# Centring the first 128 features inside the PSUM bank: a reordered opening of a fused state-space and feed-forward kernel

## The chip, the cores and the metric

The kernel runs on one core of a Trainium2 chip. TensorE (PE in the profile) multiplies matrices and writes its results to PSUM, a memory of eight banks; VectorE (DVE), ScalarE (ACT) and GpSimd (POOL) do the rest, and DMA queues, most of them issued from SyncE (SP), move data. The metric is the device time of one execution in microseconds (us).

## What is computed

The input x holds 2048 tokens of 512 features in bf16. Each token is layer-normalised; the result goes through a state-space layer (a projection, a linear recurrence over the tokens, a projection back) and through a gated feed-forward block of width 1376, and both are added to x:

```
xn = (x - mean(x)) / sqrt(var(x) + 1e-5)
ffn = (silu(xn @ w_gate) * (xn @ w_up)) @ w_down
ssm = 2 * real(h @ C^T) + xn * Dskip,  h_t = Lambda_bar * h_{t-1} + B_bar @ xn_t
out = x + ssm + ffn
```

The matmuls of the feed-forward block take the tokens transposed (features on the partitions, tokens along the free axis).

## The kernel before, in words

The work goes in four chunks of 512 tokens, each of four tiles of 128. What concerns us is the opening, lines 723 to 767, where the first three tiles (0, 1, 2) are brought into TensorE's form as fast as they arrive. The order on each engine is the order in which the code issues the instructions; semaphores are put in where one engine needs another's result.

For a tile `i` the opening does this. `sum_dve` (line 225) has VectorE add the two halves of the features with an accumulator, so that `sums[:, i]` holds each token's sum. `raw_mm` (line 237) multiplies each of the four blocks of 128 features by the identity, so that the bank `raw[i]` holds the tile transposed, not yet centred; the four blocks are called k = 0 to 3. `mean_mm` (line 242) multiplies the sums, broadcast, by `minus_mean` (the identity times -1/512), which gives minus the mean of every token on every partition, in 128 columns of another bank (`upb[1][0]` for tile 0, `upb[1][1]` for tile 1, `low` for tile 2); ScalarE copies these to `means[:, i]` in SBUF. `centered` (line 247) has VectorE add `means[:, i]` to blocks k0 to k1 of the raw bank and write them as bf16 to `xcT`, which shares its memory with the tile that the profile calls CF. The division by the standard deviation comes later, as a scale in ScalarE's reads of the products.

`up_mm(k, tiles)` (line 727) multiplies block k of the named tiles by row k of the up weights (`sw_mm`, line 500): two matmuls of 512 columns for each tile, one for each of the two groups of output features (`upb[i][0]` and `upb[i][1]`). Four rows k = 0 to 3 add up in a bank. Banks are shared: the two banks of tile 2's projections are `raw0` (the raw bank of tile 0) and `low`, and `upb[0][0]` is also `warm`, the target of `dummy` (line 698), which multiplies constants to keep TensorE busy.

The order before is: nine dummies (four of 512 columns, five of 128); sum, raw transposes and mean of tile 0, then of tile 1; five dummies of 128 columns; the centring of block 0 of tiles 0 and 1 and of blocks 1 to 3 of tile 0; row 0 of the up weights for tiles 0 and 1; sum, raw transposes and mean of tile 2; the centring of the rest of tile 1; row 1 for tiles 0 and 1; the centring of tile 2 (block 0, then blocks 1 to 3); rows 0 and 1 for tile 2; rows 2 and 3 for all three. Then follow the statistics of the layer norm on VectorE (`ln_stats`, `ln_rstd`, with the power on GpSimd), the gate projections, and ScalarE's scaled reads (`sw_up`, line 519).

The tokens of tile 0 and the up weights come on SP's queue (lines 128 and 134), one transfer for each row k; tiles 1 and 2 come on ScalarE's queue (line 131).

Of the kernel before, what the change touches and what calls it, by code (L numbers as in the profile page):

```python
# [12 lines left out]
ALU = mybir.AluOpType  # L13
# [10 lines left out]
def kernel(  # L24
# [17 lines left out]
    nc = tc.nc  # L42
    _, L, D = A_x.shape
# [8 lines left out]
    KD = D // 128  # L52
# [25 lines left out]
    def bank(shape=(128, CW), dtype=F32):  # L78
        return psum.tile(list(shape), dtype, name="ps")
# [47 lines left out]
    minus_mean = const.tile([128, 128], BF16, name="minus_mean")  # L127
# [57 lines left out]
    def by_k(ap):  # L185
        return ap.rearrange("p (k d) -> p k d", d=128)
# [30 lines left out]
    xcT, xc = CF[:, 0], CF[:, 1]  # L217
# [5 lines left out]
    sums = const.tile([128, SW], BF16, name="sums")  # L223

    def sum_dve(i, dst):
        nc.vector.scalar_tensor_tensor(out=xnT[:, NCH - 1, i, 0:HW], in0=xall[:, i, 0:HW], scalar=1.0,
                                       in1=xall[:, i, HW:D], op0=ALU.mult, op1=ALU.add, accum_out=dst)

    raw12 = [bank() for _ in range(2)]
    low, raw0 = bank(), bank()  # L230
    upb = [[bank() for _ in range(2)] for _ in range(2)] + [[raw0, low]]
    raw = [raw0, *raw12]
    gateb = [raw12, upb[0], upb[1]]
    warm = upb[0][0]
    means = ssm.tile([128, 2, CW], F32, name="pm", bufs=3)[:, 0, 0:SW * 128].rearrange("p (i t) -> p i t", t=128)

    def raw_mm(i):
        for k in range(KD):
            nc.tensor.matmul(raw[i][:, k * 128:(k + 1) * 128], lhsT=xall[:, i, k * 128:(k + 1) * 128], rhs=ident[:],  # L239
                             start=(k == 0), stop=(k == KD - 1))  # L240

    def mean_mm(i):
        lo = (*upb[1], low)[i][:, 0:128]
        nc.tensor.matmul(lo, lhsT=sums[:, i:i + 1].to_broadcast([128, 128]), rhs=minus_mean[:], start=True, stop=True)  # L244
        nc.scalar.copy(out=means[:, i, :], in_=lo)

    def centered(i, k0, k1):
        V.tensor_tensor(out=xcT[:, k0:k1, i * 128:(i + 1) * 128], in0=by_k(raw[i][:, k0 * 128:k1 * 128]),
                        in1=means[:, i, None, :].to_broadcast([128, k1 - k0, 128]), op=ALU.add)

    def runs(ap):
        return ap.rearrange("p k (i t) -> p (k i) t", t=128)
# [18 lines left out]
    V = nc.vector  # L271
# [228 lines left out]
    def sw_mm(ps, groups, gi, i, k0=0, k1=KD):  # L500
        a, b = fgroups[gi]
        for k in range(k0, k1):
            nc.tensor.matmul(ps[:, 0:(b - a) * 128], lhsT=tokens(i, k), rhs=groups[gi][:, k, 0:(b - a) * 128],  # L503
                             start=(k == 0), stop=(k == KD - 1))
# [193 lines left out]
    def dummy(ps, n, cols):  # L698
        for _ in range(n):
            nc.tensor.matmul(ps[:, 0:cols], lhsT=one.to_broadcast([128, 128]), rhs=one.to_broadcast([128, cols]),  # L700
                             start=True, stop=True)
# [22 lines left out]
    dummy(warm, 4, CW)  # L724
    dummy(warm, 5, 128)
    nc.vector.tensor_scalar(out=minus_mean[:], in0=ident[:], scalar1=-1.0 / D, scalar2=None, op0=ALU.mult)
    def up_mm(k, *tiles):
        for i in tiles:
            for gi in ((0, 1) if i < 2 else (1, 0)):
                sw_mm(upb[i][gi], U, gi, i, k, k + 1)  # L730

    def sum_mm(i):
        sum_dve(i, sums[:, i:i + 1])
        raw_mm(i)
        mean_mm(i)

    for i in range(2):
        sum_mm(i)
    dummy(warm, 5, 128)
    for i in range(2):  # L740
        centered(i, 0, 1)
    centered(0, 1, KD)
    up_mm(0, 0, 1)
    sum_mm(2)
    centered(1, 1, KD)
    up_mm(1, 0, 1)
    for k0, k1 in ((0, 1), (1, KD)):
        centered(2, k0, k1)
    for k in range(2):
        up_mm(k, 2)  # L750
    for k in range(HK, KD):
# [194 lines left out]
```

## Time and profile before

| what | value |
|---|---|
| median of three runs | 177.8 us (177.53 to 178.41) |
| the profiled execution, its own time | 178.26 us |
| span of its instructions | 176.3 us |
| TensorE busy | 172.8 us, 98% of the span |
| VectorE busy | 158.9 us, 90% |
| ScalarE busy | 102.7 us, 58% |

The profile is of one execution. Its span goes from the first to the last instruction; the rest of that execution's own time lies around it. Matmuls are pipelined: a matmul's length in the profile is the time from its start to its modelled end, and the distance from one start to the next, its pitch, is shorter. A line such as "4.83 1.91 PE L503 MATMUL ... x4" of a listing in order of time says that four matmuls issued by line 503 began at 4.83 us and ended 1.91 us later; brackets behind a row give the idle time of that engine before it and what ended it. PEld is TensorE's loading of its stationary operand. The chain of work is followed back from the last instruction, at each step to what released it.

### The profile page before, as it was taken

How to read it: one execution, taken by the hardware profiler on the slowest of the kernel's cores; microseconds unless marked ns; L12 is line 12 of the kernel's file. 1: busy time of each engine (PE TensorE's matmuls, PEld its weight loads, DVE VectorE, ACT ScalarE, POOL GpSimd, SP SyncE). 2: the span in 40 equal slices, each digit the busy share in tenths (PEclk: the TensorE clock that was granted, in tenths of full speed). 3: DMA queues.
4: the chain of work that ended last, by engine and by line, in shares of the span. 5: the costliest groups of instructions: out<-in, count | busy, mean ns of one | idle time of the engine just before them, and what ended most of it. 6: DMA issues, size and time to landing. Idle time of an engine off the chain costs nothing.

```text
span 176.3 us, 2456 instructions
## 1 busy us (share of the span) xinstructions
PE 172.8 (98%) x896; PEld 82.3 (47%) x896; DVE 158.9 (90%) x263; ACT 102.7 (58%) x186; POOL 27.1 (15%) x36
## 2 busy tenths in 40 slices
PE   8999999999999999999999999999999999999993
PEld 4444464454444464444444444445444444444542
DVE  2699999999999999899999999999999999689642
ACT  3159879895996689976044462014766662983100
POOL 5073210032000000000302500014100000530800
PEclk9999999999999999999999999999999999999999
DMA  5994979999999600220005830006410000597741
GB/s 169 366 343 63 168 148 209 283 185 307 110 203 264 170 4 0 55 57 0 2 0 109 91 42 0 0 4 67 52 22 0 2 4 0 70 174 113 81 102 60
DMA packets 34027, 18.05 MB, mean 102 GB/s; under 512 B 24512, under 2 KB 32832, under 8 KB 33888
## 3 DMA queue, kind: packets, MB, share of 16 engines
q1 hardware_dynamic: 30128, 14.26, 35.0%
q0 software_dynamic: 3456, 3.28, 14.9%
q10 hardware_dynamic: 432, 0.36, 0.6%
q8 instruction: 7, 0.11, 0.3%
q14 instruction: 4, 0.03, 0.1%
HBM read 8.33 MB, written 5.24 MB: 77 GB/s over the span
## 4 chain that ended last, share of the span: by engine, by line
PE 98%; DVE 0%; issue 0%
PE ps L459 29%; PE ps L627 20%; PE ps L640 16%; PE ps L384 16%; PE ps L503 8%; PE ps L552 3%; PE ps L801 2%; PE ps L700 2%; PE ps L617 2%; PE ps L239 1%; PE ps L244 0%; DVE xall L643 0%; PE ps L275 0%
## 5 line engine op out<-in xcount | busy, mean ns | idle before, releaser
L426 DVE TENSOR_TENSOR_SCAN g<-r_t,car,u 128x512 bf16<-128x512 f32 x24 | 28.8, 1262 | 0.0
L640 PE MATMUL ps<-CF,wt 128*128 128x512 bf16 (+2 forms) x136 | 28.5, 367 | 0.0
L384 PE MATMUL ps<-xnT,BT 128*128 128x512 bf16 x128 | 28.1, 379 | 0.0
L627 PE MATMUL ps<-wd_sb,guT 128*128 128x512 bf16 (+2 forms) x130 | 26.6, 363 | 0.0
L459 PE MATMUL ps<-xnT,wg 128*128 128x512 bf16 x96 | 24.6, 379 | 0.0
L459 PE MATMUL ps<-xnT,wu 128*128 128x512 bf16 x96 | 24.6, 379 | 0.0
L386 ACT CAST u<-ps 128x512 bf16<-128x512 f32 x32 | 18.0, 590 | 5.7 <-PE ps L384 5.2
L486 ACT CAST u<-ps 128x512 bf16<-128x512 f32 x30 | 18.0, 599 | 5.1 <-PE ps L459 5.1
L640 PEld LDWEIGHTS <-wt 128*128 128x128 bf16 x136 | 12.8, 98 | 15.1 <-DVE xall L597 0.4
L384 PEld LDWEIGHTS <-BT 128*128 128x128 bf16 x128 | 12.5, 98 | 14.9
L627 PEld LDWEIGHTS <-guT 128*128 128x128 bf16 x130 | 12.4, 98 | 13.9
L199 POOL TENSOR_TENSOR rstd<-ve,neg_half 128x1 f32<-128x1 f32 (+1 forms) x7 | 7.0, 1003 | 73.0 <-DVE ve L198 73.0
L649 ACT CAST res<-ps 128x512 bf16<-128x512 f32 x12 | 6.9, 583 | 18.6 <-PE ps L640 18.6
L589 ACT ACTIVATE xr<-xall,nb,rstd 128x512 bf16<-128x512 bf16 x16 | 11.8, 804 | 8.6 <-DVE xall L597 5.0
L650 POOL DMA_DIRECT2D out_dram<-res x12 | 10.5, 1042 | 36.0 <-ACT res L649 30.0
L459 PEld LDWEIGHTS <-wu 128*128 128x128 bf16 x96 | 9.4, 98 | 11.3
L485 ACT ACTIVATE guT<-ps 128x512 bf16<-128x512 f32 x20 | 12.0, 600 | 4.0 <-PE ps L459 3.6
L459 PEld LDWEIGHTS <-wg 128*128 128x128 bf16 x96 | 9.4, 98 | 10.6
L212 ACT ACTIVATE xn<-xall,nb,rstd 128x512 bf16<-128x512 bf16 x8 | 6.2, 816 | 8.2 <-DVE nb L202 8.2
L459 PE MATMUL ps<-xnT,w_end 128*128 128x512 bf16 x48 | 10.8, 379 | 0.0
L189 DVE BATCH_NORM_STATS2 stats<-xall 128x6 f32<-128x512 bf16 x16 | 10.8, 676 | 0.0
L394 DVE TENSOR_TENSOR pm<-g,c 128x2048 bf16<-128x2048 bf16 x8 | 9.8, 1221 | 0.1
(129 smaller groups left out, 237.8 us busy)
## 6 DMA issues: line engine op xcount, KB each, us to landing
out_dram<-in_A_x_dram SPq DMA_DIRECT2D x8, 192.0 KB, 3.2
out_dram<-res POOLq DMA_DIRECT2D x12, 128.0 KB, 3.1
out_dram<-xall POOLq DMA_DIRECT2D x3, 512.0 KB, 6.1
wd_sb<-in_B_w_down_dram SPq DMA_DIRECT2D x1, 1280.0 KB, 8.0
wu<-in_B_w_up_dram SPq DMA_DIRECT2D x4, 256.0 KB, 4.4
wg<-in_B_w_gate_dram SPq DMA_DIRECT2D x4, 256.0 KB, 5.1
xall<-in_A_x_dram SPq DMA_DIRECT2D x1, 1024.0 KB, 7.0
xall<-in_A_x_dram SPq DMA_DIRECT2D x1, 512.0 KB, 6.5
```

The costliest lines, as they stand in the source:

```text
L189: nc.vector.bn_stats(out=stats[:, n, 0, :], in_=xall[:, n, :])
L384: nc.tensor.matmul(ps[:] if c else by_k(ps[:]), lhsT=BT[:, part, k, q * 128:(q + 1) * 128], rhs=xnT[:, c, k, :] if c else xnT0[:, k], star ...
L386: nc.scalar.copy(out=u_tiles[c][:, part, q, :], in_=ps[:])
L426: V.tensor_tensor_scan(out=g()[:, part, q, :], data0=r_t[:, q:q + 1].to_broadcast([128, CW]), data1=u_tiles[c][:, part, q, :], initial=ini ...
L459: nc.tensor.matmul(ps[:fs, lo:hi], lhsT=wslice(groups, fi, k), rhs=xnT[:, c, k, lo:hi], start=(k == 0), stop=(k == KD - 1))
L485: nc.scalar.activation(out=gu(c, fi, fi + 1)[:fs, 0, :], in_=psg[:fs], func=ACT.Silu)
L486: nc.scalar.copy(out=u_pair[c][:fs, fi % 2, :], in_=psu[:fs])
L503: nc.tensor.matmul(ps[:, 0:(b - a) * 128], lhsT=tokens(i, k), rhs=groups[gi][:, k, 0:(b - a) * 128], start=(k == 0), stop=(k == KD - 1))
L589: nc.scalar.activation(out=box["xr"][:], in_=xall[:, n, :], func=ACT.Identity, scale=rstd[:, n:n + 1], bias=nb[:, n:n + 1])
L627: nc.tensor.matmul(o_tiles[n, b][:, 0:hi - lo], lhsT=gu(c, fi, fi + 1)[:, 0, i * 128:(i + 1) * 128], rhs=wd_sb[:, fi, lo:hi], start=(fi == ...
L640: nc.tensor.matmul(o[:, 0:hi - lo], lhsT=w_tiles[c][:, part, q, i * 128:(i + 1) * 128], rhs=CF[:, part, q, lo:hi], start=False, stop=(part ...
L650: nc.gpsimd.dma_start(out=out_v[:, n, lo:hi], in_=res[:, lo:hi], accum_op=ALU.add)
```

## The change

The mean of a tile is now multiplied twice: once into the first 128 columns of its raw bank, where it adds to the raw transpose of block 0 (the transposes leave the accumulation open), and once into the other bank as before. Block 0 is thereby centred in PSUM and is only copied to `xcT`: by VectorE for tile 0 (`tensor_copy`), by ScalarE for tiles 1 and 2 (`first_copy`, ahead of `mean_copy`). `centered` handles blocks 1 to 3 alone. The order is changed: the raw transposes of tile 1 stand between the two halves of tile 0's row 0, its mean behind them, then the raw transposes of tile 2, tile 1's row 0, tile 0's row 1, the mean of tile 2, tile 1's row 1, and tile 2's rows 0 and 1. The five dummies behind the means become four behind tile 0's mean. The two halves of tile 2's rows come in the order 0, 1 instead of 1, 0.

```diff
     def raw_mm(i):
         for k in range(KD):
             nc.tensor.matmul(raw[i][:, k * 128:(k + 1) * 128], lhsT=xall[:, i, k * 128:(k + 1) * 128], rhs=ident[:],
-                             start=(k == 0), stop=(k == KD - 1))
+                             start=(k == 0), stop=False)
 
     def mean_mm(i):
         lo = (*upb[1], low)[i][:, 0:128]
-        nc.tensor.matmul(lo, lhsT=sums[:, i:i + 1].to_broadcast([128, 128]), rhs=minus_mean[:], start=True, stop=True)
-        nc.scalar.copy(out=means[:, i, :], in_=lo)
-
-    def centered(i, k0, k1):
-        V.tensor_tensor(out=xcT[:, k0:k1, i * 128:(i + 1) * 128], in0=by_k(raw[i][:, k0 * 128:k1 * 128]),
-                        in1=means[:, i, None, :].to_broadcast([128, k1 - k0, 128]), op=ALU.add)
+        for to, alone in ((raw[i][:, 0:128], False), (lo, True)):
+            nc.tensor.matmul(to, lhsT=sums[:, i:i + 1].to_broadcast([128, 128]), rhs=minus_mean[:], start=alone, stop=True)
+
+    def first_copy(i):
+        nc.scalar.copy(out=xcT[:, 0, i * 128:(i + 1) * 128], in_=raw[i][:, 0:128])
+
+    def mean_copy(i):
+        nc.scalar.copy(out=means[:, i, :], in_=(*upb[1], low)[i][:, 0:128])
+
+    def centered(i):
+        V.tensor_tensor(out=xcT[:, 1:KD, i * 128:(i + 1) * 128], in0=by_k(raw[i][:, 128:D]),
+                        in1=means[:, i, None, :].to_broadcast([128, KD - 1, 128]), op=ALU.add)
...
-    def up_mm(k, *tiles):
+    def up_mm(k, *tiles, groups=range(2)):
         for i in tiles:
-            for gi in ((0, 1) if i < 2 else (1, 0)):
+            for gi in groups:
                 sw_mm(upb[i][gi], U, gi, i, k, k + 1)
 
-    def sum_mm(i):
+    def sum_to(i):
         sum_dve(i, sums[:, i:i + 1])
-        raw_mm(i)
-        mean_mm(i)
-
-    for i in range(2):
-        sum_mm(i)
-    dummy(warm, 5, 128)
-    for i in range(2):
-        centered(i, 0, 1)
-    centered(0, 1, KD)
-    up_mm(0, 0, 1)
-    sum_mm(2)
-    centered(1, 1, KD)
-    up_mm(1, 0, 1)
-    for k0, k1 in ((0, 1), (1, KD)):
-        centered(2, k0, k1)
+
+    sum_to(0)
+    raw_mm(0)
+    mean_mm(0)
+    V.tensor_copy(out=xcT[:, 0, 0:128], in_=raw[0][:, 0:128])
+    mean_copy(0)
+    dummy(warm, 4, 128)
+    sum_to(1)
+    centered(0)
+    up_mm(0, 0, groups=[0])
+    raw_mm(1)
+    up_mm(0, 0, groups=[1])
+    mean_mm(1)
+    first_copy(1)
+    mean_copy(1)
+    sum_to(2)
+    raw_mm(2)
+    up_mm(0, 1)
+    centered(1)
+    up_mm(1, 0)
+    mean_mm(2)
+    first_copy(2)
+    mean_copy(2)
+    up_mm(1, 1)
+    centered(2)
     for k in range(2):
         up_mm(k, 2)
```

## The prediction

> **What bounds the kernel now.** I read the page's first two parts and the head of its fourth, which say who is busy and which engine ends last.
>
> ```profile
> PE 172.8 (98%) x896; PEld 82.3 (47%) x896; DVE 158.9 (90%) x263; ACT 102.7 (58%) x186; POOL 27.1 (15%) x36
> PE   8999999999999999999999999999999999999993
> PEclk9999999999999999999999999999999999999999
> PE 98%; DVE 0%; issue 0%
> ```
>
> TensorE is never idle to speak of, and the chain that ended last lies on it from end to end. So a pause that an edit opens in the matmul stream, or a matmul that it adds, comes out at the end in full, and work taken from VectorE or ScalarE pays only if a matmul was waiting for it. The edit lies in the first 9 us, so I read next the chain of work in order of time (start, length, piece). A piece's length divided by its count is the pitch of its matmuls; its start is set by ends and lies some 0.2 us behind the instruction's own.
>
> ```profile
> 0.78 2.40 PE ps L700 x9
> 3.18 0.03 issue
> 3.21 0.61 PE ps L239 x4
> 3.82 0.15 PE ps L244
> 3.98 0.43 PE ps L239 x4
> 4.40 0.11 PE ps L244
> 4.51 0.53 PE ps L700 x5
> 5.04 1.71 PE ps L503 x4
> 6.75 0.40 PE ps L239 x4
> 7.15 0.06 PE ps L244
> 7.21 3.05 PE ps L503 x14
> 25.01 13.81 PE ps L384 x64
> ```
>
> A 512-column matmul has a pitch of 1.71/4 = 0.43 us in the first group of up projections (L503), and of 13.81/64 = 0.216 us later; a 128-column one 0.53/5 = 0.107 at first and 0.06 in the mean of tile 2 (L244). So TensorE runs at half its rate until some 6.9 us and doubles there, although the page's clock row shows the full clock throughout. In the slow stretch a lost microsecond costs only half of one later, as long as the doubling stays where it is.
>
> Third, the same stretch in the order of instructions, engine by engine (start, length of the merged group, in brackets the idle time before it and its releaser).
>
> ```profile
> 3.69 0.29 PE L244 MATMUL ps<-minus_mean,sums 128*128 128x128 bf16 x1
> 4.20 0.31 PE L244 MATMUL ps<-minus_mean,sums 128*128 128x128 bf16 x1
> 4.30 0.74 PE L700 MATMUL ps<-const-bfloat16-1.0 128*128 128x128 bf16 x5
> 4.83 1.91 PE L503 MATMUL ps<-wu,CF 128*128 128x512 bf16 x4
> 6.54 0.61 PE L239 MATMUL ps<-ident,xall 128*128 128x128 bf16 x4
> 6.97 0.24 PE L244 MATMUL ps<-minus_mean,sums 128*128 128x128 bf16 x1
> 3.19 0.42 DVE L226 SCALAR_TENSOR_TENSOR xnT<-xall 128x256 bf16<-128x256 bf16 x1 [1.65 <-DMA xall<-in_A_x_dram]
> 4.31 0.29 DVE L248 TENSOR_TENSOR CF<-ps,pm 128x128 bf16<-128x128 f32 x1 [0.32 <-ACT pm L245]
> 5.52 0.41 DVE L226 SCALAR_TENSOR_TENSOR xnT<-xall 128x256 bf16<-128x256 bf16 x1
> 7.54 0.76 DVE L248 TENSOR_TENSOR CF<-ps,pm 128x128 bf16<-128x128 f32 x2 [1.13 <-ACT pm L245]
> 7.75 0.55 DVE L248 TENSOR_TENSOR CF<-ps,pm 128x384 bf16<-128x384 f32 x1
> 4.01 0.27 ACT L245 COPY pm<-ps 128x128 f32<-128x128 f32 x1 [0.94 <-PE ps L244]
> 7.24 0.27 ACT L245 COPY pm<-ps 128x128 f32<-128x128 f32 x1 [2.43 <-PE ps L244]
> 8.35 0.55 PEld L503 LDWEIGHTS <-CF 128*128 128x128 bf16 x4 [0.34 <-DVE CF L248]
> ```
>
> These give the hand-overs: mean matmul to ScalarE 0.03 us (3.69 + 0.29 to 4.01), ScalarE to VectorE 0.03 (4.01 + 0.27 to 4.31), VectorE to weight load 0.05 (7.75 + 0.55 to 8.35). The five dummies cover the wait for tile 0's first features: those are ready at 4.31 + 0.29 + 0.05 = 4.65, the dummies end at 4.83. **The mark for the sum** is 8.35: there row 1 of tile 2 starts, the last matmul that waits for a centring. Behind it the stream is gap-free.
>
> **The change, part by part.** Removed: one 128-column dummy, and three VectorE additions of 128 columns. Added: three 128-column mean matmuls into the raw banks, one VectorE copy, two ScalarE copies. Nothing is issued to a DMA queue, so SP's and POOL's queues are not touched. Net on TensorE: two matmuls of 128 columns, 2 x 0.06 = +0.12 us at the full rate, since what is added ahead of the doubling pushes other matmuls behind it. The rest is waits, so I lay the new order out, with the doubling held at 6.9.
>
> *Tile 0.* The mean into the raw bank starts at 3.69 and ends at 3.98; the second one follows at 3.80, the four dummies from 3.90 to 4.33. The copy starts on VectorE at 4.01. The trace has no copy of this shape; its bounds are
>
> ```profile
> 10.35 0.17 DVE L279 COPY prm<-ps 128x12 f32<-128x12 f32 x1
> L122 SPq DMA_DIRECT2D wu<-in_B_w_up_dram x2: 412/422/432, 1.2 to 1.7; - x2
> DMA to landing us min/median/max: 3.1/3.7/4.3
> ```
>
> 0.17 us (12 columns) below and 0.55 (the 384-column addition) above; I take 0.29, the addition of the same shape. Then the weight load can go at 4.01 + 0.29 + 0.05 = 4.35. Row 0 of the up weights (the first of these two transfers) lands at 1.2 + 3.1 = 4.3, and its hand-over lets it go at about 4.38 anyway, so a copy quicker than 0.29 gains nothing. TensorE pauses 0.05 us and starts the first up projection at 4.38 rather than 4.83. The copy stands in VectorE's queue ahead of tile 1's sum: that starts about 0.21 later (as 7.75 stands to 7.54), at 4.22 instead of 3.56, and releases its mean 0.5 later (as 3.69 to 3.19), near 4.7; tile 1's mean now waits behind two halves and four transposes, so it costs nothing.
>
> *Tile 1.* 4.38 + 0.43 + 4 x 0.107 + 0.43 = 5.66: its mean pair starts, then the raw transposes of tile 2, until 6.30. ScalarE's first copy ends at 5.66 + 0.31 + 0.03 + 0.27 = 6.28 (0.31 is what the mean at 4.20 took in a running stream at the slow rate), so tile 1's row 0 starts at 6.33, pause 0.03. Its second half straddles the doubling and ends at 7.03; row 1 of tile 0 (landed at 1.7 + 4.3 = 6.0, centred near 5.1) ends at 7.46.
>
> *Tile 2.* Its mean pair starts only now, at 7.46, where before it started at 6.97. Row 1 of tile 1 runs to 8.00. ScalarE's first copy of tile 2 starts at 7.46 + 0.24 + 0.03 = 7.73 and ends at 8.00, so row 0 goes at 8.05 (pause 0.05) and ends at 8.48. Its halves are turned round, raw bank first; the low bank is free of the mean copy when its turn comes at 8.27, or within 0.05 of that. The mean copy queues behind the first copy on ScalarE and ends at 8.27, or at 8.17 if the two overlap by 0.1, about as VectorE's do (7.54 + 0.29 against 7.75); VectorE's centring takes 0.55, and row 1 of tile 2 can go at 8.80 to 8.90. TensorE has been idle since 8.48. **This pause of about 0.37 us is the largest term**: before, six matmuls of 512 columns lay between tile 2's mean and this row, now four, and one more ScalarE copy lies in the way.
>
> Sum: 8.85 - 8.35 = **+0.50 us**, of which +0.12 is matmuls, 0.37 + 0.05 pauses at the full rate, and the rest is small pauses at the slow rate against rounding. Nothing behind takes it back:
>
> ```profile
> 8.21 0.69 DVE L189 BATCH_NORM_STATS2 stats<-xall 128x6 f32<-128x512 bf16 x1
> 9.39 0.58 POOL L199 TENSOR_TENSOR rstd<-ve,neg_half 128x1 f32<-128x1 f32 x1 [5.84 <-DVE ve L198]
> 10.63 2.42 ACT L523 ACTIVATE u<-ps,rstd 128x512 bf16<-128x512 f32 x4 [3.12 <-PE ps L503]
> ```
>
> VectorE's statistics start when the centring lets them, 0.5 later; POOL's first rstd ends near 10.5 instead of 9.97, still ahead of ScalarE's read, which moves to 11.1 with the matmuls.
>
> The profiled execution (176.3 us span, 178.26 in all, so 2.0 around it) becomes 176.8 and 178.76. It lies 0.46 over the median of 177.8 of the three runs, and I have one trace: the doubling may lie elsewhere in the others. With the doubling at 5.4 the same working gives: changed kernel, tile 1's mean at 5.53, its row 0 at 6.12 (pause 0.26), tile 2's mean at 6.98, the mark 1.39 later (as 8.85 - 7.46) at 8.37; before, tile 2's mean at 6.20 and the mark 1.38 later at 7.58; so +0.79. Between +0.50 and +0.79 I take +0.6, nearer to the trace at hand: **178.4 us**.
>
> **Rivals.**
>
> *The pauses put the doubling off (slower).* Before, the matmuls run from 3.21 with no pause over 0.05 until the rate doubles 3.7 us later. If a pause starts that count anew, the one that ends at 4.38 puts the doubling at 8.07: tile 2's mean starts at 8.04, the mark is at 8.04 + 1.39 = 9.43, +1.08, 178.9. The one at 6.33 would put it at 10.0: the mark is reached at half rate at 9.96, +1.6, 179.4. It decides from a doubling after some 7.7 on. For it: the doubling came only after the gap at 3.2. Against: transposes and mean had a pause of 0.05 at 3.64 (3.21 + 4 x 0.107 to 3.69), no shorter than the new ones, and it did not start anything anew. [...]
>
> *The up weights land later.* Before, row 0 could land 0.45 later unnoticed; now every 0.1 us shows, at half price ahead of the doubling. Landing at 4.7 gives +0.7 to +1.0, 178.5 to 178.8. For it: the cover is gone. Against: the queue ahead of it is unchanged.
>
> *Tile 2's centring is hidden after all.* If ScalarE's two copies overlap well or the banks come free earlier, only the matmuls are left, +0.12: 177.9. Against: the chain from mean to row is 1.38 us in the trace as it stands, and 4 x 0.216 cover 0.86.
>
> *The doubling comes earlier, as useful matmuls start at 4.38 (faster).* With the full rate from 4.4 on, tile 1's mean starts at 5.04, row 0 of tile 1 at 5.63, tile 2's mean at 6.51, the mark is 7.90: -0.45, 177.35. Against: the stream up to 4.3 is the same in both.
>
> **How the numbers follow.** Forecast 0.62 (178.0 to 178.8), late doubling 0.14, late weights 0.08, hidden centring 0.10, early doubling 0.06. The range goes from 177.5 (hidden centring, less the 0.4 that single runs scatter: 177.53 to 178.41) to 179.3 (late doubling at 178.9 and the same 0.4). Within 0.5% is 0.89 us, about what a measurement of this kernel can tell from no change. Slower by more: the late doubling 0.14, half the late weights 0.04, the upper end of the forecast 0.08, so 0.26. Faster by more: part of the early doubling, 0.04. Same: 0.70.
>
> **What would show it.** In the changed trace: the first up projection at about 4.4 with a pause under 0.1; tile 1's sum near 4.2; tile 2's first half of row 0 with hardly a wait; a weight load that waits 0.3 to 0.4 us for VectorE's 384-column addition of tile 2; the last row 0.5 us later than before, and from there on equal distances. A pitch of 0.43 beyond 7.7 would be the late doubling. If there is no wait ahead of row 1 of tile 2, the largest term was wrong.

## The result and the profile after

The changed kernel took 178.53 us (median of 13 runs, 178.27 to 179.07), the kernel before 177.55 in the same sessions (13 runs, 177.28 to 178.44). The ratio is 1.0044, with a 95% interval of 1.0029 to 1.0059: slower by 0.78 us (0.51 to 1.05). That is clear of scatter; the estimate lies below 0.5%, the upper end of its interval a little above. (The medians lie 0.98 apart, the means of the same runs 0.80.) The profiled execution of the changed kernel took 178.55, with a span of 176.5 us.

The chain of work of the changed kernel, in order of time (start, length, piece; pieces named after TensorE's lines 509 and 245 are the up projections and the means):

```profile
1.20 3.84 DMA wu<-in_B_w_up_dram
5.04 0.04 issue
5.08 0.38 PE ps L509
...
5.99 0.28 ACT CF L248
6.27 0.05 issue
6.31 1.04 PE ps L509 x4
7.35 0.07 PE ps L245
7.42 0.02 issue
7.44 0.27 ACT CF L248
7.71 0.18 ACT pm L251
7.88 0.02 issue
7.91 0.57 DVE CF L254
8.48 0.05 issue
8.53 1.90 PE ps L509 x8
```

Before, this stretch was TensorE alone. Now the chain leaves TensorE three times: for the transfer of the first up weights, for ScalarE's first copy of tile 1, and from tile 2's mean by way of both ScalarE copies and VectorE's centring to the mark of the prediction, row 1 of tile 2, at 8.52. TensorE's own rows say how long it stood:

```profile
3.88 0.63 PE L706 MATMUL ps<-const-bfloat16-1.0 128*128 128x128 bf16 x4
5.08 0.38 PE L509 MATMUL ps<-wu,CF 128*128 128x512 bf16 x1 [0.57 <-DMA wu<-in_B_w_up_dram]
5.30 0.38 PE L239 MATMUL ps<-ident,xall 128*128 128x128 bf16 x4
...
7.19 0.28 PE L245 MATMUL ps<-minus_mean,sums 128*128 128x128 bf16 x2
7.30 1.07 PE L509 MATMUL ps<-wu,CF 128*128 128x512 bf16 x4
8.53 1.25 PE L509 MATMUL ps<-wu,CF 128*128 128x512 bf16 x5 [0.16 <-DVE CF L254]
```

The bracket counts from the modelled end of the matmul before; by the pitch the wait is longer. The last of the four matmuls ends at 7.30 + 1.07 = 8.37 and, with a length of 0.38 and a pitch of 0.22, would have let the next start at 8.21: TensorE waited 0.32 us for tile 2's centring. And the first up projection started at 5.08, although the dummies let go at 4.30.

Two things differ between this execution and that of before which the edit does not touch, and which the runs below show to vary between executions of one kernel. The four raw transposes at 5.30 take 0.38 us together, where a slow stretch shows 0.61 to 0.63: the rate had doubled by then, not at 6.9. And row 0 of the up weights, issued at 1.20 as before, landed 3.8 us later, not 3.1.

Where the time went is settled by one subtraction. The first gate projection and the last instruction on VectorE, in the trace of before:

```profile
11.44 1.89 PE L503 MATMUL ps<-wg,CF 128*128 128x512 bf16 x8
...
173.67 0.29 DVE L643 TENSOR_TENSOR xall<-ps,jidx 128x128 bf16<-128x128 f32 x1 [0.25 <-PE ps L640]
```

and in the changed kernel:

```profile
11.61 1.67 PE L509 MATMUL ps<-wg,CF 128*128 128x512 bf16 x7
...
173.84 0.29 DVE L649 TENSOR_TENSOR xall<-ps,jidx 128x128 bf16<-128x128 f32 x1 [0.25 <-PE ps L646]
```

The distance is 162.23 in both, and between 162.22 and 162.23 in all thirteen traces of this document. So what the opening does to the time can be read from the start of the gate projections alone, and nothing later gives any of it back. These two traces differ by only 0.17, because the one of before had its doubling at 6.9, later than any other with the same transfers; the second traces below are the better pair.

### The profile page after: what moved, and what is told of

The parts are those of the page before. It is cut to its first block, busy times and chain, and to the rows that moved or that the text cites. A ratio compares the mean times of both kernels' runs of the same rounds, so it can differ in the third digit from the quotient of the medians.

```text
span 176.5 us, 2460 instructions
## 1 busy us (share of the span) xinstructions
PE 172.2 (98%) x898; PEld 81.8 (46%) x898; DVE 158.5 (90%) x261; ACT 103.0 (58%) x188; POOL 27.1 (15%) x36
## 4 chain that ended last, share of the span: by engine, by line
PE 95%; DMA 2%; DVE 0%; ACT 0%; SPq 0%; issue 0%
PE ps L465 29%; PE ps L633 20%; PE ps L646 16%; PE ps L390 16%; PE ps L509 8%; PE ps L558 3%; DMA wu<-in_B_w_up_dram 2%; PE ps L817 2%; PE ps L623 2%; DVE CF L254 0%; ACT CF L248 0%; SPq L128 0%; DVE xall L649 0%; PE ps L239 0%; ACT pm L251 0%
```

## The experiments

**The theory** ("order"): the loss is in the order of the work. Tile 2's mean is issued too late for its centring, and the first up weights have lost their cover. **Rivals**: the centring itself costs the time (three mean matmuls, ScalarE copies), or the pauses put off the doubling of TensorE's rate ("late clock"). Times below are medians beside runs of the kernel before on the same chip; a ratio of 1.001 is 0.18 us.

**The changed kernel again.** No edit.

> The changed kernel once more, for a second trace of it and its time beside the three variants on the same chip. All theories: 0.5 to 1.0 over the kernel before. Theory 'order': wherever the doubling and the first up weights lie this time, TensorE waits 0.3 to 0.6 us ahead of row 1 of tile 2 and, if row 0 of the up weights lands after 4.35, from the dummies' end until then. Rival 'late clock': a pitch of 0.43 us beyond 7.7 in this or the other trace.

178.45 us, ratio 1.0046 (1.0022 to 1.0070): +0.82. In this execution the rate doubled near 6.1 and the weights came in time:

```profile
3.84 0.63 PE L706 MATMUL ps<-const-bfloat16-1.0 128*128 128x128 bf16 x4
4.32 0.61 PE L509 MATMUL ps<-wu,CF 128*128 128x512 bf16 x1
...
7.12 0.28 PE L245 MATMUL ps<-minus_mean,sums 128*128 128x128 bf16 x2
7.24 1.07 PE L509 MATMUL ps<-wu,CF 128*128 128x512 bf16 x4
8.46 1.90 PE L509 MATMUL ps<-wu,CF 128*128 128x512 bf16 x8 [0.15 <-DVE CF L254]
```

The first up projection starts at 4.32, 0.06 after the dummies let go (3.84 + 4 x 0.107 = 4.27); from tile 2's mean to the mark it takes 8.46 - 7.12 = 1.34 us, as in the first trace (8.53 - 7.19). No pitch of 0.43 is left beyond 6.1 in either trace. That speaks against "late clock".

**The kernel before again.** No edit.

> The kernel before, unchanged, against itself: a ratio of 1.000 within 0.0015, and a second trace of it, for where the doubling of TensorE's rate and the landing of row 0 lie this time. Theory 'order': with the doubling earlier than 6.9 the mark (row 1 of tile 2) lies earlier than 8.35, by half of the difference as long as no wait comes between.

177.60 us, ratio 0.9992 (0.9974 to 1.0010). The trace shows what one execution of before had hidden:

```profile
4.81 1.43 PE L503 MATMUL ps<-wu,CF 128*128 128x512 bf16 x4
6.07 0.39 PE L239 MATMUL ps<-ident,xall 128*128 128x128 bf16 x4
6.29 0.22 PE L244 MATMUL ps<-minus_mean,sums 128*128 128x128 bf16 x1
6.35 3.21 PE L503 MATMUL ps<-wu,CF 128*128 128x512 bf16 x14
...
10.75 2.54 PE L503 MATMUL ps<-wg,CF 128*128 128x512 bf16 x11
```

The transposes of tile 2 take 0.39, so the rate had doubled by 6.07 (near 5.6 by the pitches), and the gate projections start at 10.75 instead of 11.44. The same kernel gains 0.69 us by a doubling 1.3 us earlier: half of it, as expected.

In the second trace of the changed kernel the gate projections start at 11.55, 0.80 later than here. Some 0.25 of that is chance: its rate doubled 0.5 us later, and that counts half. The estimate of 0.55 that is left agrees with the terms of the prediction: 0.32 for the wait at the mark, 0.11 for the two added matmuls of 128 columns at 0.056, and small pauses.

**Tile 2's mean earlier.** The changed kernel with one line moved:

```diff
     raw_mm(2)
+    mean_mm(2)
     up_mm(0, 1)
     centered(1)
     up_mm(1, 0)
-    mean_mm(2)
     first_copy(2)
```

> The changed kernel with one edit: tile 2's mean pair is issued straight behind tile 2's raw transposes instead of behind tile 0's row 1. Theory 'order' (the loss is the wait ahead of row 1 of tile 2, because tile 2's mean comes too late, plus the wait for the first up weights, whose cover is gone): the wait of some 0.4 to 0.5 us ahead of row 1 of tile 2 goes, the time falls by 0.4 to 0.5 from the changed kernel's and stays 0.1 to 0.5 over the kernel before. Rival 'centring itself' (the loss is the added matmuls and ScalarE copies): the time stays within 0.15 of the changed kernel's, some 0.8 over before. Rival 'late clock' (pauses put off the doubling of TensorE's rate): also as the changed kernel, and a pitch of 0.43 us still beyond 7.7 us.

177.78 us, ratio 0.9999 (0.9985 to 1.0014): 0.67 under the changed kernel's 178.45 of the same session, and level with before. The direction is as expected, the gain larger than the 0.4 to 0.5 that was expected, and nothing is left of the 0.1 to 0.5 over before. By chance this trace has the conditions of the first one of the changed kernel, an early doubling and late weights, so the two can be laid side by side:

```profile
3.68 0.52 PE L706 MATMUL ps<-const-bfloat16-1.0 128*128 128x128 bf16 x4
5.05 0.38 PE L509 MATMUL ps<-wu,CF 128*128 128x512 bf16 x1 [0.85 <-DMA wu<-in_B_w_up_dram]
...
6.28 3.63 PE L509 MATMUL ps<-wu,CF 128*128 128x512 bf16 x16
...
11.10 2.11 PE L509 MATMUL ps<-wg,CF 128*128 128x512 bf16 x9
```

Sixteen up projections follow one another from 6.28 with 3.63 us for all: (3.63 - 0.38)/15 = 0.217 each, no wait ahead of row 1 of tile 2. The first up projection starts 0.03 earlier than in the changed kernel, the gate projections 0.51 earlier (11.10 against 11.61). So the moved line is worth 0.48 us here: 0.32 is the wait at the mark, and most of the rest is the mean pair itself (0.11), which now falls into the time that TensorE waits for ScalarE's first copy of tile 1 anyway (0.24 in the first trace of the changed kernel). What makes the medians differ by 0.67 instead of 0.48 is not shown by one trace of each. The centring itself is no cause: all its instructions are still there.

**The centring alone, in the order of before.** From the first sum to tile 2's centring this kernel reads:

```python
    for i in range(2):
        sum_to(i)
        raw_mm(i)
        mean_mm(i)
    V.tensor_copy(out=xcT[:, 0, 0:128], in_=raw[0][:, 0:128])
    mean_copy(0)
    first_copy(1)
    mean_copy(1)
    dummy(warm, 4, 128)
    centered(0)
    up_mm(0, 0, 1)
    sum_to(2)
    raw_mm(2)
    mean_mm(2)
    first_copy(2)
    mean_copy(2)
    centered(1)
    up_mm(1, 0, 1)
    centered(2)
```

> Only the centring in PSUM, in the order of the kernel before: means into the raw banks, first copies by VectorE (tile 0) and ScalarE, four dummies behind both means; row 0 for tiles 0 and 1, then tile 2's transposes and means, and so on. Theory 'order': within 0.1 of the kernel before (-0.05 to +0.1), since 0.12 of added matmuls stands against the shorter way to the first row. Rival 'centring itself': about +0.8 over before, as the changed kernel. Rival 'late clock': within 0.1 of before as well, since the stream has no pause.

177.68 us, ratio 0.9987 (0.9968 to 1.0007). As the theory had it; the rival "centring itself" falls with this too. This kernel also has the changed kernel's four dummies and its turned halves of tile 2's rows, so these are not the loss either.

**The order alone, with the centring of before.** The new order of the calls; `mean_mm` and `centered` as before.

> Only the new order, with the centring of before (one mean matmul for each tile, ScalarE copies the mean, VectorE adds it to block 0 and then to blocks 1 to 3). Theory 'order': the wait for a centring is longer than in the changed kernel, since block 0 needs two hand-overs again: 0.9 to 1.3 over the kernel before, 0.2 to 0.5 over the changed one. Rival 'centring itself': within 0.15 of before. Rival 'late clock': over before by 1 us or more, with a pitch of 0.43 us beyond 7.7.

178.51 us, ratio 1.0054 (1.0029 to 1.0078): +0.96 over before, as expected, but only 0.06 over the changed kernel where 0.2 to 0.5 was expected; the intervals do not tell these apart. The trace shows the longer waits:

```profile
4.63 0.58 PE L503 MATMUL ps<-wu,CF 128*128 128x512 bf16 x1 [0.25 <-DVE CF L248]
...
6.39 1.04 PE L503 MATMUL ps<-wu,CF 128*128 128x512 bf16 x4 [0.46 <-DVE CF L248]
...
8.16 2.15 PE L503 MATMUL ps<-wu,CF 128*128 128x512 bf16 x9 [0.25 <-DVE CF L248]
```

Three waits for VectorE, of 0.25 to 0.46 by the brackets, where the changed kernel has one of 0.16. So the centring in PSUM shortens the waits that the order makes, but does not remove the last one.

**The changed kernel without the four dummies** (`dummy(warm, 4, 128)` taken out).

> The changed kernel without the four dummies behind tile 0's mean. Theory 'order': TensorE waits there for the copy and for the weights with or without them, so the time is within 0.15 of the changed kernel's (0.5 to 1.0 over before). Rival 'late clock' (a pause puts off the doubling of the rate): the pause of 0.4 us and more at 3.9 moves the doubling to 7.7 or later, and the time rises by 0.5 to 1.1 over the changed kernel's.

178.29 us, ratio 1.0023 (0.9996 to 1.0049): +0.41, a little under the 0.5 to 1.0 that was expected, in an interval that holds both the changed kernel's +0.78 and no loss at all. The rise that "late clock" asked for did not come.

```profile
3.49 0.40 PE L245 MATMUL ps<-minus_mean,sums 128*128 128x128 bf16 x2
4.17 0.61 PE L509 MATMUL ps<-wu,CF 128*128 128x512 bf16 x1 [0.28 <-DMA wu<-in_B_w_up_dram]
...
5.63 0.59 PE L239 MATMUL ps<-ident,xall 128*128 128x128 bf16 x4
6.09 1.04 PE L509 MATMUL ps<-wu,CF 128*128 128x512 bf16 x4
```

TensorE stood for 0.5 us behind tile 0's means (from 3.49 + 2 x 0.107 to 4.17), and the rate doubled near 6.05 all the same. In this trace a pause of this size did not put the doubling off to 7.7 or later.

**Centring alone, order of before, no dummies behind the means.**

> Centring in PSUM in the order of before, and none of the four dummies behind the two means. Theory 'order': the first up projection starts when row 0 of the weights and the copy are there, 0 to 0.4 earlier than with dummies; waits behind it take most of that back, so 0 to 0.2 under the kernel before. Rival 'late clock': the pause puts off the doubling, 0.3 to 1.0 over before.

177.52 us, ratio 0.9990 (0.9973 to 1.0007). The next wait took the gain back:

```profile
4.31 1.04 PE L509 MATMUL ps<-wu,CF 128*128 128x512 bf16 x4
...
6.32 3.18 PE L509 MATMUL ps<-wu,CF 128*128 128x512 bf16 x14 [0.64 <-DMA wu<-in_B_w_up_dram]
```

Row 0 starts at 4.31, 0.5 earlier than in before, and then row 1 of the weights is not there yet.

**Three attempts at an earlier row 0.** First in the changed kernel, row 0 as SP's first transfer:

```diff
-    nc.sync.dma_start(out=xall[:, 0, :], in_=x_v[:, 0, :])
+    load_row(nc.sync, wu01, wu_v, 0)
+    nc.scalar.dma_start(out=xall[:, 0, :], in_=x_v[:, 0, :])
...
-    for k in range(KD):
+    for k in range(1, KD):
         load_row(nc.sync, wu01, wu_v, k)
```

> The changed kernel with row 0 of the up weights as the first transfer on SP's queue, and tile 0's tokens moved to ScalarE's queue ahead of tiles 1 and 2. In the traces so far row 0 landed at 4.34 (before), 5.04 and 4.19 (changed, twice), 5.03 (early mean), 4.25 and 4.24. Theory 'order': the share of the loss that is the uncovered weights goes, the wait for tile 2's centring stays: row 0 lands some 0.4 us earlier, TensorE starts the first up projection within 0.1 of the dummies' end, and the time is 0 to 0.3 below the changed kernel's, 0.4 to 0.7 over before. If the weights' share is nothing: as the changed kernel, about 0.8 over before, though row 0 lands early.

179.97 us, ratio 1.0111 (1.0063 to 1.0160): a miss by 1.3 us and more. The tokens of tile 0 became the late ones:

```profile
4.14 0.61 PE L240 MATMUL ps<-ident,xall 128*128 128x128 bf16 x4 [0.96 <-DMA xall<-in_A_x_dram]
...
7.48 1.91 PE L510 MATMUL ps<-wu,CF 128*128 128x512 bf16 x4
9.19 0.42 PE L246 MATMUL ps<-minus_mean,sums 128*128 128x128 bf16 x2
```

Tile 0's transposes start at 4.14, where those of the kernels with the unedited transfers start between 3.02 and 3.23, and the up projections still run at a pitch of 0.43 at 7.48 (four in 1.91). This says nothing on the weights' share. The same in the kernel without dummies:

> The same, and row 0 of the up weights first on SP's queue, tile 0's tokens on ScalarE's. Theory 'order': 0.05 to 0.25 under the kernel before, less scatter, as the late landings of row 0 no longer count. If tile 0's tokens come later through that, the time rises by what they are late, at half price.

180.24 us, ratio 1.0120 (1.0072 to 1.0168), in the same way: tile 0's transposes start at 4.24. The half price that was expected for late tokens, some 0.5 us, is missed by far (+2.1): the rate doubled only near 9.5. Then, in the changed kernel, row 0 in two transfers:

```diff
+    for f0 in (0, FE // 2):
+        nc.sync.dma_start(out=wu01[:, 0, f0:f0 + FE // 2], in_=wu_v[:, 0, f0:f0 + FE // 2])
-    for k in range(KD):
+    for k in range(1, KD):
         load_row(nc.sync, wu01, wu_v, k)
```

> The changed kernel with row 0 of the up weights fetched in two transfers of half the features, the first half alone being what the first up projection needs; the other transfers follow 0.4 us later than they did. Theory 'order' with an uncovered first row: in traces of the same opening row 0 was issued at 1.20 and landed 2.9 to 3.1 us later in most, but 3.8 later in two (the changed kernel, early mean); the first half should land by 4.2 in all, the wait behind the dummies be under 0.15, and the time be 0 to 0.3 under the changed kernel's, that is 0.4 to 0.7 over before. If the first half lands as late as the whole row, or row 1 is late instead, as the changed kernel or over it.

179.20 us, ratio 1.0072 (1.0048 to 1.0096): +1.28 instead of 0.4 to 0.7. The first half came in time, and TensorE waited for row 1 instead:

```profile
4.10 0.61 PE L511 MATMUL ps<-wu,CF 128*128 128x512 bf16 x1
...
6.89 0.59 PE L511 MATMUL ps<-wu,CF 128*128 128x512 bf16 x2 [0.29 <-DMA wu<-in_B_w_up_dram]
...
8.66 1.69 PE L511 MATMUL ps<-wu,CF 128*128 128x512 bf16 x7 [0.15 <-DVE CF L256]
```

Yet most of the rise over the changed kernel is elsewhere. The gate projections start at 11.75, only 0.14 to 0.20 later than in the two traces of the changed kernel. From the start of the last VectorE addition to the end of the span it takes 3.10 us here, and 2.67 to 2.69 in the traces without half transfers. These 0.43 us are there in both kernels with the additional transfer and in no other; what fills them was not shown, and they say nothing on when the weights land.

And in the kernel without dummies:

> Centring in PSUM in the order of before, no dummies behind the means, and row 0 of the up weights in two halves. Theory 'order': as psum_old_no_dummies (0.16 under before) or up to 0.2 better, if a late row 0 cost it anything. If row 1 comes 0.4 later through the additional transfer, it is the next wait, and the time is 0.1 to 0.3 over before.

178.52 us, ratio 1.0043 (1.0016 to 1.0069): +0.76, over the 0.1 to 0.3 that was expected for a late row. There the second half, issued at 1.66, landed 4.10 later, and TensorE waited for it until 5.80 (its rows are shown in the last section), and the end again takes 3.13 us, 0.44 longer; without that the rise is some 0.3. So the share that late weights have in the changed kernel's loss was not isolated: each edit that hurried row 0 delayed something else, and the half transfers lengthened the end as well. What can be said comes from the traces as they fell. In the nine with the unedited transfers, row 0 was issued at 1.20 and landed 2.9 to 3.1 us later in seven and 3.8 in two. Landing at 5.0 reaches past 4.83, where before starts its up projections, by only 0.2, and past the 4.3 of the changed kernel by 0.7.

No version was shown to beat the kernel before: the centring in PSUM with the order of before is at 0.9987 and 0.9990, and both intervals include 1.

## Why the prediction was right

Right: +0.6 was forecast and +0.78 (0.51 to 1.05) measured, the time of 178.4 against 178.53, by the mechanism that was named.

- **The first up projection at 4.38 with a pause of 0.05**: 4.32 with 0.06 in the second trace. In the first it was 5.08, which is the rival of the late weights. It had a chance of 0.08 and occurred in two of nine traces with the same transfers, so it is commoner in single executions than that; how much of the median it makes is not shown.
- **The pause ahead of tile 1's row 0, 0.03 with the late doubling and 0.26 with the early one**: under 0.1 in the second trace (doubling near 6.1) and 0.24 in the first (before 5.1).
- **From tile 2's mean to the mark, 1.39**: 1.34 in both traces. The copies on ScalarE overlap, by 0.1.
- **The wait at the mark, 0.37**: 0.32. Taking it away by one moved line brought 0.48 between two traces of like conditions, and 0.67 between medians.
- **The mean matmuls and copies, small**: shown. The centring alone costs nothing that can be measured (0.9987).
- **Nothing behind takes it back**: shown to 0.01 us by the distance of 162.22 to 162.23 in every trace. The last row itself came only 0.17 later than in the first trace of before and not 0.5, since the doublings differ.
- **The copy on VectorE, 0.29**: 0.29.
- **The doubling held at 6.9, with +0.79 for an earlier one**: the sum of +0.50 was leaned on a doubling that turned out the latest of the nine openings (4.0 to 6.9). A doubling near 5.4 is nearer to the usual, and the measured +0.78 lies at that end. But its interval takes in both sums, and the second traces of the two kernels give an estimate of 0.55 for equal doublings. So that 178.4 came so close is partly luck: it was added to a median of 177.8, and the larger set of runs has 177.55.
- **Late clock, 0.14**: did not occur in any trace with pauses of up to 0.5 us ahead of the doubling.
- **Early doubling, 0.06**: in the first trace the rate had doubled before the first up projection, so not because useful matmuls started at 4.38, and the execution was no faster: the weights were late and the wait at the mark remained.
- **Hidden centring, 0.10**: not in this kernel; the moved mean makes it true, and brings the time back to that of before.

## What to carry to other kernels

On an engine that is never idle, count for each hand-over how many matmuls lie between the instruction that starts the chain and the one that needs its end: 1.34 us of chain wants six matmuls of 0.216, and a reorder that leaves four shows the rest, less the mean matmuls' own 0.11, as waits, whatever it saves on the way. A moved start also needs the data that the old start had time to wait for. And before leaning on a sum from one trace, ask what in it changes from execution to execution; here the doubling of the rate alone moves the same kernel by 0.7 us.

## What the runs showed of the hardware beyond that

TensorE's rate doubled between 3.6 and 6.9 us in the traces whose matmuls started on time, with openings that are the same up to 3.0. The earliest, in the order-of-before kernel with two half transfers, is seen by the raw transposes:

```profile
3.15 0.61 PE L241 MATMUL ps<-ident,xall 128*128 128x128 bf16 x4
3.62 0.28 PE L247 MATMUL ps<-minus_mean,sums 128*128 128x128 bf16 x2
3.74 0.39 PE L241 MATMUL ps<-ident,xall 128*128 128x128 bf16 x4
...
4.24 0.39 PE L511 MATMUL ps<-wu,CF 128*128 128x512 bf16 x1
5.80 0.81 PE L511 MATMUL ps<-wu,CF 128*128 128x512 bf16 x3 [1.18 <-DMA wu<-in_B_w_up_dram]
```

Four transposes take 0.61 ahead of the doubling and 0.39 behind it. It lies near 3.6, 2.8 us behind the first dummy at 0.78, and the wait from 4.62 to 5.80 did not undo it: the three up projections behind that wait take 0.81, a pitch of (0.81 - 0.38)/2 = 0.215. What sets the moment between 3.6 and 6.9 was not shown.

In the two kernels whose first tokens came 1 us late, the pitch was still 0.43 at 9.4 us, and the rate doubled near 10.1 and 9.5. Ahead of it TensorE had stood for more than 1 us, from 2.98 to 4.14 and 4.24. Only two traces show this, but all twelve executions of the two kernels took 179.48 us or more, where 21 of the 23 of the kernel before in that session took 178.39 or less: at least 1.1 between them, of which tokens 1 us late at half price explain 0.5. So the late doubling was probably there in most of them. That the pause is its cause was not tested by itself.

In these two kernels tile 0's tokens (128 KB) went out on ScalarE's queue at 0.74, together with row 0 (256 KB) on SP's, and landed 3.3 us later in the first; in the second the transposes that wait for them start 0.10 later than in the first (4.24 against 4.14). As SP's first transfer, issued at the same time, they took 2.4 in the trace of before. Whether the other queue or the larger transfer beside it did this was not separated.
